# Moving waits and loads in the gradient stages of a fused attention and MLP backward kernel

## The chip, the cores and the metric

The kernel runs on one core of one Trainium2 chip. The metric is the time of one execution on the device in microseconds (us); the time before is the median of three runs. Engines are named as in the profile: PE (TensorE), DVE (VectorE), ACT (ScalarE), POOL (GpSimd) and SP (SyncE, which here only issues DMAs). Each engine works its instructions in the order in which the program lists them, and so does each engine's queue of DMA issues: an instruction that waits holds up all behind it on that engine.

## What is computed

The reference is a forward pass and its gradients (2048 tokens, width 512, 32 heads of 16, hidden width 1792, bf16):

```
x = A_x;  xn = layernorm(x)
s = attention(xn, wqkv, wo)
g = silu( gelu(layernorm(xn) @ w1 + b1) @ w2 + b2 )
out = x + s * g
_out, _vjp = jax.vjp(f, A_x, A_wqkv, A_wo, B_w1, B_b1, B_w2, B_b2)
returns out and the gradients of all seven inputs for grad_out
```

The outputs are, in order: `out` (out_0), dx (out_1), dwqkv (out_2), dwo (out_3), dw1 (out_4), db1 (out_5), dw2 (out_6), db2 (out_7).

## The kernel before

The program has three parts. `Pre` does the forward work of everything but the attention and leaves in DRAM what the gradients need. `attention_core` does scores, softmax and their gradients head pair by head pair; it takes most of the time. `Grads.run` does the rest, and the change lies in it alone. Rows of tokens are cut into 16 tiles t of 128 (NT), the width into 4 pieces of 128 (IC), the hidden width into 14 pieces fc of 128 (FC). The order of instructions is written out by hand, engine by engine, and waits follow from the tiles' uses. A new tile under an old tag waits for all uses of the old one.

`Grads.run` goes through these stages, in which every full matmul is 128x128 by 128x512:

1. **so and dwo** (t = 2 to 15). `emit_so(t)` makes four matmuls; DVE multiplies the result twice, into `dm_all` and into one of two rows "t13", which POOL adds to x one tile later (`flush_adds`) and stores from two double rows "ot". `emit_oT(t+2)` and `emit_dmT` are PE transposes into two PSUM buffers, which ACT copies out (L564, L707). `load_s1(q)` loads the factors of two tiles into one of four buffers and so waits on SP for POOL's adds of an earlier pair. At t = 9, 11, 13 and 14 `emit_dwo` makes one of four weight gradients: 16 matmuls over `Oall` and `dso_all` (L719), evacuated by ACT (L714) into one of three buffers "ob", and stored by POOL's queue.
2. **dw2** (fc = 0 to 13). `emit_dw2(fc)`: 16 matmuls (L728) over `dm_all` and `hgr[fc % 4]`, a piece of the hidden activations that a transposing DMA (`load_hg`, L698) brings in. `load_hg(fc + 4)` waits for the end of `emit_dw2(fc)`.
3. **dwq and dwkv** (i = 0 to 11). Four gradients over `xn1` and `dQall` (L812), then two halves of four over `xn1` and `dKVn[half]` (L820). Each half needs four transposing DMAs (`load_dkv`, L783). `xn1` (L800) has the buffer "xg", which `dso_all` had before.
4. **dh and dy** (four groups of each). dh needs `w2T`, 14 transposing DMAs (`load_w2T`, L780), dy needs `w1T` (L853); both change the chunks of `gp` in place or read them.
5. **dw1 and dx**. Three pieces of dw1 (L973), then 16 rows of dx (13 matmuls each, L1002 to L1006), then the last piece of dw1.

Beside stages 1 to 3 runs **slope**: the derivative of gelu for 16 chunks n of up to 128x2048, in place in `gp`. It is a list of 49 steps, which `slope_step(m)` takes m at a time. A chunk goes through a square on ACT (`sl_sq`, L654), `d1` and `d2` on DVE (two passes each, L658 to L664), two sigmoids on ACT (`sl_sg`, L668 and L669; the first one writes over `gp`, which `d2` reads) and `d3` on DVE (three passes, L673 to L675). Its inputs come through `load_h1` (L644).

A row of dx goes through `ln_a` (ACT sum L891, DVE L892 to L895, with a product tile from `row("ot")`), an ACT pass into one of four rows `r2r` (L1009), an add with the rows of grad_out, `dor` (L1011: POOL, and DVE for rows 14 and 15), and a store from SP's queue (L1014). The tile of the add comes from `row("ot")` too: that helper hands out two buffers in turn, and `ln_a` asks it once for each row as well. Ahead of the stores of rows 1 and 5 SP issues four loads each (`load_dx`).

Of the kernel before, what the change touches and what calls it, by code (L numbers as in the profile page):

```python
# [8 lines left out]
bf16 = mybir.dt.bfloat16  # L9
f32 = mybir.dt.float32  # L10
ACT = mybir.ActivationFunctionType
ALU = mybir.AluOpType
# [3 lines left out]
S, D, H, DH, F = 2048, 512, 32, 16, 1792  # L16
# [460 lines left out]
class Grads:  # L477
# [119 lines left out]
    def run(self):  # L597
        nc, k, tc, ctx = self.nc, self.k, self.tc, self.ctx
# [7 lines left out]
        ld = nc.sync.dma_start  # L606
        tr = nc.sync.dma_start_transpose
        st = nc.gpsimd.dma_start
        V = nc.vector

        def slot(tag, shape, name, dtype=bf16):
            return slots.tile(shape, dtype, name=name, tag=tag)
# [18 lines left out]
        def ob_tile():  # L631
            i = no[0] % 3
            no[0] += 1
            return slot(f"ob{i}", [128, D], "ob_w")
# [7 lines left out]
        def load_h1(tg, ci):  # L642
            c0, cn = CH[ci]
            ld(out=gpc(tg, ci), in_=h1v[:, c0:c0 + cn, tg * 512:(tg + 1) * 512])  # L644
# [43 lines left out]
        def slope_step(m=1):  # L688
            for _ in range(m):
                if slope_ops:  # L690
                    slope_ops.pop(0)[1]()
# [5 lines left out]
        def load_hg(fc):  # L697
            tr(out=hgr[:, fc % 4], in_=k.HGT_s[fc * 128:fc * 128 + 128, :])  # L698
# [4 lines left out]
        def emit_dmT(t):  # L703
            pt = self.pT([128, IC, 128], bf16, "dm_tp")
            for b in range(IC):
                nc.tensor.transpose(pt[:, b, :], dm_all[:, t, b * 128:(b + 1) * 128], k.ident_bf[:])
            nc.scalar.copy(out=dmT[:, :, t * 128:(t + 1) * 128], in_=pt[:])  # L707
            nc.tensor.matmul(psdb2[0:1, :], lhsT=ones_bf[:, 0:1], rhs=dm_all[:, t, :], start=(t == 0), stop=(t == NT - 1))

        def evac(out, in_, e):  # L710
            if e:
                nc.vector.tensor_copy(out=out, in_=in_)
            else:
                nc.scalar.copy(out=out, in_=in_)  # L714

        def emit_dwo(ac):
            ps = self.pA([128, D], f32, "ps_dwo")
            for t in range(NT):
                nc.tensor.matmul(ps[:], lhsT=k.Oall[:, t, ac * 128:(ac + 1) * 128], rhs=dso_all[:, t, :],  # L719
                                 start=(t == 0), stop=(t == NT - 1))  # L720
            ob = ob_tile()
            evac(ob[:], ps[:], 0)
            st(out=out_3[ac * 128:(ac + 1) * 128, :], in_=ob[:])

        def emit_dw2(fc):
            ps = self.pA([128, D], f32, "ps_dw2")
            for t in range(NT):
                nc.tensor.matmul(ps[:], lhsT=hgr[:, fc % 4, t, :], rhs=dm_all[:, t, :], start=(t == 0), stop=(t == NT - 1))  # L728
            ob = ob_tile()
            evac(ob[:], ps[:], 0)  # L730
            st(out=out_6[fc * 128:(fc + 1) * 128, :], in_=ob[:])
# [11 lines left out]
        for t in range(2, NT):  # L743
            self.emit_so(t)
            if t + 2 < NT:
                self.emit_oT(t + 2)
            while nd < t and nd <= 2 * (t - 3) + 1:
                emit_dmT(nd)
                nd += 1
            if t == 3:  # L750
                self.load_s1(5)
                ld(out=dso_all[:, 0:8], in_=dsov[:, 0:8])
            if t == 5:
                self.load_s1(6)
                ld(out=dso_all[:, 8:16], in_=dsov[:, 8:16])
                load_h1(0, 2)
                slope_step(1)
            if t == 7:
                self.load_s1(7)
                load_hg(0)  # L760
                slope_step(1)
            if t in (9, 11, 13, 14):
                i = (9, 11, 13, 14).index(t)
                emit_dwo(i)
                (load_hg(i + 1) if i < 3 else load_h1(1, 1))
                (load_h1(0, 3) if i == 0 else load_h1(1, 0) if i == 2 else None)
                slope_step(1 + i % 2)
        self.flush_adds()
        while nd < NT:
            emit_dmT(nd)  # L770
# [4 lines left out]
        xn1 = slot("xg", [128, NT, D], "xn1")  # L775
# [3 lines left out]
        def load_w2T(f2):  # L779
            tr(out=w2T[:, f2], in_=self.B_w2[f2 * 128:f2 * 128 + 128, :])  # L780

        def load_dkv(h, rc):
            tr(out=dKVn[h][:, :, rc, :], in_=k.dKVT_s[512 * h + rc * 128:512 * h + rc * 128 + 128, :])  # L783
# [4 lines left out]
        xnv = k.XN_s.rearrange("(t p) d -> p t d", p=128)  # L788


        nw = 0
        for fc in range(FC):
            emit_dw2(fc)
            if fc + 4 < FC:
                load_hg(fc + 4)
            if fc % 2 == 0 and fc >= 2:
                load_h1(1 + (fc + 2) // 8, ((fc + 2) // 2) % 4)
            if fc in (3, 5, 7, 9):
                q = (fc - 3) // 2
                ld(out=xn1[:, 4 * q:4 * q + 4], in_=xnv[:, 4 * q:4 * q + 4])  # L800
            if fc in (0, 2, 4, 6, 8):
                load_w2T(nw)
                nw += 1
            if fc >= 11:
                load_dkv(0, fc - 11)
            slope_step(1 + fc % 2)


        def emit_dwq(ic):
# [74 lines left out]
        def ln_a(ps, xhat, rstd_col):  # L884
            junk = self.row("oT", [128, D], bf16)
            r = self.row("t13")
            prod = self.row("ot", [128, D], bf16)
            sc = lns[nln[0] % 4] if nln[0] < 4 else slot(f"lns{nln[0] % 4}", [128, 4], "lns", f32)
            nln[0] += 1
            s1, s2, nb = sc[:, 0:1], sc[:, 1:2], sc[:, 2:3]  # L890
            nc.scalar.activation(out=junk[:], in_=ps, func=ACT.Copy, accum_out=s1)  # L891
            nc.vector.tensor_tensor_reduce(out=prod[:], in0=ps, in1=xhat, scale=-1.0 / D, scalar=0.0, op0=ALU.mult, op1=ALU.add,  # L892
                                           accum_out=s2)
            nc.vector.scalar_tensor_tensor(out=r[:], in0=xhat, scalar=s2, in1=ps, op0=ALU.mult, op1=ALU.add)
            nc.vector.tensor_scalar(out=nb, in0=s1, scalar1=-1.0 / D, scalar2=rstd_col, op0=ALU.mult, op1=ALU.mult)  # L895
            return r, nb
# [50 lines left out]
        for h4 in range(4):  # L947
            tr(out=dQT[:, 4 * h4:4 * h4 + 4].rearrange("c t b s -> c (t b) s"),
               in_=k.dQall[:, 4 * h4:4 * h4 + 4, :].rearrange("s t c -> s (t c)"))
# [5 lines left out]
        xn_all = self.pO.tile([128, NT, D], bf16, name="xn_all", tag="dQall")  # L955
        dor = slot("hgw", [128, 3, 4, D], "dor")
        r2r = slot("gp1", [128, 4, D], "r2r", f32)
        nc.vector.reduce_sum(out=db1f[:], in_=db1acc[:], axis=AX.X)

        nx = [5]  # L960
# [29 lines left out]
        def load_dx(q):  # L990
            for j in range(2):
                ld(out=R[j][:, :, 512 * q:512 * q + 512], in_=rv[:, 4 * j:4 * j + 4, 512 * q:512 * q + 512])
            ld(out=xn_all[:, 4 * q:4 * q + 4], in_=xnv[:, 4 * q:4 * q + 4])
            ld(out=dor[:, q % 3], in_=self.gov[:, q * 4:q * 4 + 4, :])
# [5 lines left out]
        for t in range(NT):  # L1000
            ps = self.pA([128, D], f32, "ps_dxa")
            nc.tensor.matmul(ps[:], lhsT=k.ident_bf[:], rhs=dxm_all[:, t, :], start=True, stop=False)  # L1002
            for cc in range(IC):
                nc.tensor.matmul(ps[:], lhsT=dQT[:, t, cc, :], rhs=wT[:, cc, :, :], start=False, stop=False)
            for rc in range(8):
                nc.tensor.matmul(ps[:], lhsT=R[rc // 4][:, rc % 4, t * 128:(t + 1) * 128], rhs=wT[:, 4 + rc, :, :], start=False, stop=(rc == 7))  # L1006
            r, nb = ln_a(ps[:], xn_all[:, t, :], k.rstd1[:, t:t + 1])
            r2 = r2r[:, t % 4, :]
            nc.scalar.activation(out=r2, in_=r[:], func=ACT.Identity, bias=nb, scale=k.rstd1[:, t:t + 1])  # L1009
            dx = self.row("ot", [128, D], bf16)  # L1010
            (V if t >= 14 else nc.gpsimd).tensor_tensor(out=dx[:], in0=r2, in1=dor[:, (t // 4) % 3, t % 4, :], op=ALU.add)  # L1011
            if t in (1, 5):
                load_dx(2 + t // 4)
            ld(out=self.o1[t * 128:(t + 1) * 128, :], in_=dx[:])  # L1014
        emit_dw1(3)


# [448 lines left out]
```

## Time and profile before

| what | value |
|---|---|
| time, median of 3 runs (lowest to highest) | 2246.61 us (2244.68 to 2248.53) |
| span of the profiled execution, first to last instruction | 2242.4 us |
| instructions | 74217 |
| PE busy | 2160.1 us (96%) |
| DVE busy | 1912.2 us (85%) |
| ACT busy | 1734.5 us (77%) |
| POOL busy | 606.8 us (27%) |
| mean granted TensorE clock | 0.991 |
| DMA moved | 461.15 MB, mean 206 GB/s |

The profiled execution's own time is given by its span; no other time of it is on record, and the median of the runs lies 4.2 us above it. The engines work beside each other, so that their busy times do not add up to the span. The shares are averages over stages with different limits; the stages that the change touches lie in the last 370 us, from about 1876 us on.

In a timeline row stand start, length, engine, line, operation, output and inputs, shape and count, and in brackets the idle time of the engine just before with what ended it. "SPq" is SP's queue of DMA issues; its length is the time that the issue held the queue, not the transfer.

### The profile page before, as it was taken

Reading aid. Unit: us, or ns where it says so; the run is one execution under the profiler, and the core shown is the slowest. Engines: PE = TensorE matmul, PEld = TensorE weight load, DVE = VectorE, ACT = ScalarE, POOL = GpSimd, SP = SyncE. Lnnn points to the kernel's source line nnn. Section 1 sums busy time; section 2 is a strip of 40 time slices with the busy share of each in tenths; the row PEclk is TensorE's granted clock in tenths of the full one; section 3 lists DMA queues with packets and bytes.
Section 4 is the critical chain, followed back from the end, with each engine's and each line's share of the span. In section 5 each row is a group of like instructions: output and inputs, shape, how many; then the busy total and the mean of one; then the engine's idle time right before and its main releaser. Section 6 shows DMA issues by size and latency. Waiting matters only on the chain.

```text
span 2242.4 us, 74217 instructions
## 1 busy us (share of the span) xinstructions
PE 2160.1 (96%) x30690; PEld 1205.0 (54%) x30690; DVE 1912.2 (85%) x3626; ACT 1734.5 (77%) x2481; POOL 606.8 (27%) x1387
## 2 busy tenths in 40 slices
PE   6998999999999999999999999999999999989996
PEld 3444555555555555555555555555555554434443
DVE  6676799999999999999999999999999997777623
ACT  4764788888888888888888888888888886674213
POOL 4276413122222222131222222221312224310012
PEclk9999899999999999999999999999999999999998
DMA  7786999999999999999999999999999999899972
GB/s 238 242 273 197 184 199 194 202 200 203 195 203 194 200 197 206 196 199 200 198 203 197 203 192 204 199 199 197 204 196 190 204 205 273 194 257 240 233 222 94
DMA packets 1421747, 461.15 MB, mean 206 GB/s; under 512 B 1334622, under 2 KB 1405662, under 8 KB 1421408
## 3 DMA queue, kind: packets, MB, share of 16 engines
q1 hardware_dynamic: 1406880, 424.67, 99.3%
q0 software_dynamic: 12944, 30.16, 5.4%
q8 instruction: 240, 3.93, 0.8%
q10 hardware_dynamic: 1584, 1.57, 0.2%
q14 instruction: 99, 0.81, 0.1%
HBM read 62.79 MB, written 64.75 MB: 57 GB/s over the span
## 4 chain that ended last, share of the span: by engine, by line
PE 86%; DMA 5%; DVE 2%; issue 2%; ACT 2%; POOL 2%; SPq 0%; POOLq 0%; DVEq 0%; ACTq 0%
PE tT L1166 23%; PE d L1104 14%; PE X L1196 10%; PE Z L1280 10%; PE X L1199 5%; PE X L1203 5%; PE s L1082 2%; PE ps_m L367 2%; PE ps_dy L902 2%; PE ps_dw L973 2%; PE ps_dh L868 2%; PE ps_h L352 2%; DMA out_dram<-ot 2%; PE XT L1222 1%; PE ps_dwkv L820 1%
## 5 line engine op out<-in xcount | busy, mean ns | idle before, releaser
L1121 DVE TENSOR_TENSOR gts<-d,ets 128x512 bf16<-128x512 f32 x2048 | 1363.2, 684 | 101.0 <-ACT ek L1178 20.3
L1091 ACT ACTIVATE ets<-s 128x1024 bf16<-128x1024 f32 x1024 | 1048.7, 1024 | 198.5 <-PE s L1082 95.2
L1166 PE MATMUL tT<-ident_bf,ets 128*128 128x128 bf16 x7168 | 568.9, 219 | 16.7 <-ACT ek L1178 6.9
L1166 PEld LDWEIGHTS <-ets 128*128 128x128 bf16 x7168 | 445.5, 97 | 242.0 <-issue 240.2
L1178 ACT COPY ek<-tT 128x448 f32<-128x448 f32 (+2 forms) x1024 | 501.6, 490 | 8.1 <-DVE ek L1178 6.9
L1104 PE MATMUL d<-QDT,KVT 32*128 32x512 bf16 x2048 | 458.6, 385 | 0.0
L1082 PE MATMUL s<-QDT,KVT 32*128 32x512 bf16 x2048 | 401.6, 381 | 3.4 <-ACT ets L1091 3.2
L1104 PEld LDWEIGHTS <-KVT 32*128 32x128 bf16 x2048 | 145.4, 91 | 323.9 <-issue 323.9
L1196 PE MATMUL X<-ets,NAT 128*32 128x256 bf16 x4096 | 300.6, 284 | 0.1
L1203 PE MATMUL X<-gts,NAT 128*17 128x256 bf16 x4096 | 290.0, 273 | 0.0
L1199 PE MATMUL X<-ets,Lc 128*32 128x256 bf16 x4096 | 289.9, 273 | 0.0
L1340 POOL COPY tick<-gts 1x2 bf16<-1x2 bf16 x205 | 36.2, 176 | 606.1 <-DVE gts L1121 606.1
L1280 PE MATMUL Z<-gk,W 128*32 128x512 bf16 x2048 | 197.8, 379 | 1.0 <-DVE acc L1294 1.0
L1280 PE MATMUL Z<-ek,W 128*32 128x512 bf16 x1792 | 198.6, 379 | 0.0
L1245 POOL TENSOR_TENSOR W<-NATQq,rL 128x128 bf16<-128x128 bf16 x64 | 25.4, 397 | 526.1 <-DVE rL L1244 443.3
L1196 PEld LDWEIGHTS <-NAT 128*32 128x32 bf16 x4096 | 106.2, 93 | 110.8 <-issue 11.4
L1082 PEld LDWEIGHTS <-KVT 32*128 32x128 bf16 x2048 | 139.0, 91 | 12.5 <-issue 9.5
L1178 DVE COPY ek<-tT 128x64 f32<-128x64 f32 (+1 forms) x576 | 132.4, 230 | 5.5 <-POOL KVT L50 4.2
L1280 PEld LDWEIGHTS <-W 128*32 128x32 bf16 x4096 | 109.7, 97 | 11.4 <-issue 1.5
L1199 PEld LDWEIGHTS <-Lc 128*32 128x32 bf16 x4096 | 107.9, 96 | 0.0
L1203 PEld LDWEIGHTS <-NAT 128*17 128x17 bf16 x4096 | 103.6, 92 | 3.1
L1280 PE MATMUL Z<-ekd,W 128*32 128x512 bf16 x256 | 97.0, 379 | 0.0
(244 smaller groups left out, 2339.3 us busy)
## 6 DMA issues: line engine op xcount, KB each, us to landing
gk<-gts SPq DMA_TRANSPOSE x512, 5.1
H1T_s<-h1r SPq DMA_DIRECT2D x28, 256.0 KB, 4.3
HGT_s<-hgT SPq DMA_DIRECT2D x8, 896.0 KB, 4.6
DH_s<-stg SPq DMA_DIRECT2D x12, 512.0 KB, 3.1
hch<-DH_s SPq DMA_DIRECT2D x12, 512.0 KB, 4.7
gp<-H1T_s SPq DMA_DIRECT2D x9, 512.0 KB, 5.4
out_dram<-ob_w POOLq DMA_DIRECT2D x36, 128.0 KB, 4.1
NAT_s<-NS SPq DMA_DIRECT2D x4, 1056.0 KB, 6.2
```

Of the source, the lines that this page charges most:

```text
L352: nc.tensor.matmul(ps[:], lhsT=w1_sb[:, ic, fc * 128:(fc + 1) * 128], rhs=yT[:, ic, g * 512:(g + 1) * 512], start=(ic == 0), stop=(ic == I ...
L367: nc.tensor.matmul(ps[:], lhsT=hgT[:, g % 2, fc, t4 * 128:(t4 + 1) * 128], rhs=w2_sb[:, fc, :], start=(fc == 0), stop=(fc == FC - 1))
L1082: nc.tensor.matmul(s[:, hj, :], lhsT=op["KVT"][r:r + 32, kb * 128:(kb + 1) * 128], rhs=op["QDT"][r:r + 32, qc * 512:(qc + 1) * 512], start ...
L1091: nc.scalar.activation(out=st_et[g][:, :, :, a[1] % 4, :].rearrange("k b h q -> k h b q"), in_=cur["s"][:].rearrange("k h (b q) -> k h b q ...
L1104: nc.tensor.matmul(d[:], lhsT=op["KVT"][r:r + 32, kb * 128:(kb + 1) * 128], rhs=op["QDT"][r:r + 32, qc * 512:(qc + 1) * 512], start=True, ...
L1121: nc.vector.tensor_tensor(out=gts[:, kb % 2, hj, :].rearrange("k (b q) -> k b q", b=4), in0=st_d.pop((g, hj))[:].rearrange("k (b q) -> k b ...
L1166: nc.tensor.transpose(t[:, i, :], et[:, b // 2, b % 2, kk, :], ident_bf[:])
L1178: copy(out=blk[j]["Ek"][kb // 4][:, kb % 4, lo:hi].rearrange("q i k -> q (i k)").bitcast(f32), in_=st_T[g][:, lo:hi].rearrange("q i k -> q ...
L1196: nc.tensor.matmul(X[r:r + 32, 0:256], lhsT=NATt[:, kb, hj, 1:33], rhs=ev, start=(kb == 0), stop=False, skip_group_check=True, tile_positi ...
L1199: nc.tensor.matmul(X[r:r + 32, 256:512], lhsT=Lc[:], rhs=ev, start=False, stop=False, skip_group_check=True, tile_position=(0, r))
L1203: nc.tensor.matmul(X[r:r + 17, 256:512], lhsT=NATt[:, kb, hj, 0:17], rhs=gv, start=False, stop=(kb == 15), skip_group_check=True, tile_pos ...
L1280: nc.tensor.matmul(Z[r:r + 32, :], lhsT=WT[j % 2][1 - part][:, qb, hj, :], rhs=mv, start=(part == 0 and qb == 0), stop=(part == 1 and qb = ...
```

## The change

Four edits, all in `Grads.run`:

- The add of a dx row writes one of eight rows of a tile of its own, `dxr`, in the buffer "gp2" (chunks that dh and dy of group 2 used before), and no longer a tile from `row("ot")`.
- In the so/dwo stage the slope steps at t = 5 and t = 7 and those behind each `emit_dwo` go; `emit_dwo` itself takes 1, 2, 1 and 2 steps between its matmuls and its evacuation. In dw2 the steps for fc = 0 to 3 are 2 each (before 1, 2, 1, 2).
- The first two of the four loads of `xn1` are issued ahead of the dw2 loop, the other two at fc = 9 and 11 (before: at fc = 3, 5, 7, 9).
- `load_w2T` is called at fc = 10 to 13 (before: fc = 0, 2, 4, 6, 8). The rest follow in the dwq/dwkv loop as before, two for each i from 4 to 8 until there are 14.

```diff
@@ emit_dwo
                 nc.tensor.matmul(ps[:], lhsT=k.Oall[:, t, ac * 128:(ac + 1) * 128], rhs=dso_all[:, t, :],
                                  start=(t == 0), stop=(t == NT - 1))
+            slope_step((1, 2, 1, 2)[ac])
             ob = ob_tile()
             evac(ob[:], ps[:], 0)
@@ loop over t
                 load_h1(0, 2)
-                slope_step(1)
             if t == 7:
                 self.load_s1(7)
                 load_hg(0)
-                slope_step(1)
             if t in (9, 11, 13, 14):
...
                 (load_h1(0, 3) if i == 0 else load_h1(1, 0) if i == 2 else None)
-                slope_step(1 + i % 2)
@@ dw2
         nw = 0
+        for q in range(2):
+            ld(out=xn1[:, 4 * q:4 * q + 4], in_=xnv[:, 4 * q:4 * q + 4])
         for fc in range(FC):
             emit_dw2(fc)
...
-            if fc in (3, 5, 7, 9):
-                q = (fc - 3) // 2
+            if fc in (9, 11):
+                q = (fc - 5) // 2
                 ld(out=xn1[:, 4 * q:4 * q + 4], in_=xnv[:, 4 * q:4 * q + 4])
-            if fc in (0, 2, 4, 6, 8):
+            if fc >= 10:
                 load_w2T(nw)
                 nw += 1
             if fc >= 11:
                 load_dkv(0, fc - 11)
-            slope_step(1 + fc % 2)
+            slope_step(1 + (fc % 2 or fc < 4))
@@ dx
+        dxr = slot("gp2", [128, 8, D], "dxr")
...
-            dx = self.row("ot", [128, D], bf16)
-            (V if t >= 14 else nc.gpsimd).tensor_tensor(out=dx[:], in0=r2, in1=dor[:, (t // 4) % 3, t % 4, :], op=ALU.add)
+            dx = dxr[:, t % 8, :]
+            (V if t >= 14 else nc.gpsimd).tensor_tensor(out=dx, in0=r2, in1=dor[:, (t // 4) % 3, t % 4, :], op=ALU.add)
...
-            ld(out=self.o1[t * 128:(t + 1) * 128, :], in_=dx[:])
+            ld(out=self.o1[t * 128:(t + 1) * 128, :], in_=dx)
```

## The prediction

> **What bounds the kernel now.** I read the page first, then the waits, the chain of waits and the timelines of the last 370 us, since the diff touches only the gradient stages after the attention loop.
>
> ```profile
> span 2242.4 us, 74217 instructions
> POOL ot L1011 <- DMA out_dram<-ot: 35.6, 13, 6.6
> DVE ot L1011 <- DMA out_dram<-ot: 11.1, 1, 11.1
> 2223.74 1.16 POOL ot L1011
> 2224.92 1.68 DMA out_dram<-ot
> 2226.82 1.16 POOL ot L1011
> 2221.96 3.54 PE L973 MATMUL ps_dw<-hch,y_all 128*128 128x256 bf16 x31 [0.29 <-DVE t L894]
> ```
>
> The waits of the last 73 us (total, times, longest) and three steps of the chain: each dx row is added on POOL into one of two "ot" buffers, but the product of `ln_a` takes every other one, so all dx rows share a single buffer. Add, store, landing, next add: 2226.82 - 2223.74 = 3.08 us a row at best, more where a load lies ahead of the store. PE's last matmul ends at 2221.96 + 3.54 = 2225.5, and 17 us of the span follow it. That is the first bound.
>
> The second is the weight-gradient stages before it, where PE sets the end but has gaps:
>
> ```profile
> 1897.90 0.38 PE L562 MATMUL o_tp<-ident_bf,Oall 128*128 128x128 bf16 x4 [3.36 <-ACT oT L564]
> 1899.42 1.89 PE L571 MATMUL ps_so<-wo_sb,oT 128*128 128x512 bf16 x4
> 1906.49 1.89 PE L719 MATMUL ps_dwo<-dso_all,Oall 128*128 128x512 bf16 x8 [0.55 <-DMA dso_all<-DSO_s]
> 1914.69 0.38 PE L562 MATMUL o_tp<-ident_bf,Oall 128*128 128x128 bf16 x4 [3.73 <-ACT oT L564]
> 1916.04 4.97 PE L719 MATMUL ps_dwo<-dso_all,Oall 128*128 128x512 bf16 x16
> 1920.85 1.03 PE L571 MATMUL ps_so<-wo_sb,oT 128*128 128x512 bf16 x4
> 1922.57 1.04 PE L571 MATMUL ps_so<-wo_sb,oT 128*128 128x512 bf16 x4
> 1936.38 34.71 PE L728 MATMUL ps_dw<-dm_all,hgr 128*128 128x512 bf16 x160
> 1972.38 3.63 PE L728 MATMUL ps_dw<-dm_all,hgr 128*128 128x512 bf16 x16 [1.29 <-DMA hgr<-HGT_s]
> 1978.32 7.28 PE L728 MATMUL ps_dw<-dm_all,hgr 128*128 128x512 bf16 x32 [2.32 <-DMA hgr<-HGT_s]
> 1988.59 3.63 PE L728 MATMUL ps_dw<-dm_all,hgr 128*128 128x512 bf16 x16 [2.99 <-DMA hgr<-HGT_s]
> 2005.87 27.79 PE L820 MATMUL ps_dwkv<-dKVn,xn 128*128 128x512 bf16 x128
> ```
>
> PE's timeline (start, length, line, count, idle before and its releaser). In the so/dwo stage (to 1936.4) two gaps of over 3 us wait for a ScalarE copy; in dw2 three gaps, 1.29 + 2.32 + 2.99 = 6.6 us, wait for transposed loads of hgr. Full speed is 34.71 / 160 = 0.217 us a matmul, so 3.47 us for a weight gradient of 16 and, from 1920.85 to 1922.57, 1.72 us for one row of so work.
>
> **Part one: dx rows in eight buffers.** Nothing is added: the same 16 adds and stores. What is late next is the layer-norm chain of ScalarE and VectorE:
>
> ```profile
> 2219.01 0.81 ACT L1009 ACTIVATE r2r<-t,lns,rstd 128x512 f32<-128x512 f32 x1 [1.73 <-DVE lns L895]
> 2222.13 0.81 ACT L1009 ACTIVATE r2r<-t,lns,rstd 128x512 f32<-128x512 f32 x1 [1.73 <-DVE lns L895]
> 2233.13 0.69 DVE L1011 TENSOR_TENSOR ot<-r2r,dor 128x512 bf16<-128x512 f32 x1 [11.10 <-DMA out_dram<-ot]
> 2236.28 0.69 DVE L1011 TENSOR_TENSOR ot<-r2r,dor 128x512 bf16<-128x512 f32 x1 [0.94 <-ACT r2r L1009]
> 2239.16 0.42 DVE L712 CAST ob_w<-ps_dw 128x256 bf16<-128x256 f32 x1 [1.85 <-DMA out_dram<-ob_w]
> ```
>
> Row 14's r2 is ready at 2222.13 + 0.81 = 2222.9; its add, which runs on VectorE, waits until 2233.13 for the store of row 13. With eight buffers it starts at about 2223.0, 10.1 us sooner. Rows come every 3.12 us (2222.13 - 2219.01), more than the 1.16 us POOL add needs, and eight rows are 25 us, longer than any store here (6.6 us was the longest wait for one), so no buffer is late again. Behind the add stand row 15, the four evacuations of dw1(3) and their stores, from 2233.13 to the end 9.3 us, all unchanged: PE's end at 2225.5 is ahead of row 15's add (2236.28 - 10.1 = 2226.2). So this part gives **10.1 us** (9 to 10.5).
>
> **Part two: slope's passes ahead of dwo's evacuation.**
>
> ```profile
> 1893.67 3.71 ACT L654 ACTIVATE sl<-gp 128x2048 bf16<-128x2048 bf16 x2 [1.19 <-DMA gp<-H1T_s]
> 1909.02 1.28 ACT L668 ACT_TABLE_LOAD   x1
> 1910.31 1.91 ACT L668 ACTIVATE gp<-sl 128x2048 bf16<-128x2048 bf16 x1
> 1912.26 1.91 ACT L669 ACTIVATE sl<-sl 128x2048 bf16<-128x2048 bf16 x1
> 1915.01 0.69 DVE L663 TENSOR_SCALAR sl<-sl 128x2048 bf16<-128x2048 bf16 x1
> 1915.73 1.23 DVE L664 TENSOR_TENSOR sl<-sl,gp 128x2048 bf16<-128x2048 bf16 x1
> 1896.30 0.46 SPq L755 DMA_DIRECT2D dso_all<-DSO_s  x1
> ```
>
> The squares (3.71 us) made the 3.36 gap; table load and sigmoids (5.1 us) made the 3.73 gap. Both now run in the shade of dwo's matmuls. Four things take part of it back.
> (1) The first gap's gain is not kept. Without it PE reaches dwo(0) at about 1898.8 (so(7) ended at 1897.90 - 3.36 = 1894.5, then two and a half rows of 1.72) and its eighth matmul at 1900.5, but the second half of dso_all, issued at 1896.30 behind a wait for POOL's add of row 5, still lands at 1906.4. PE idles 5.9 us there.
> (2) That idle time costs clock. After the 3.36 us gap four matmuls took 1.89 instead of 1.03 us, after 3.73 sixteen took 4.97 instead of 3.63; after 2.99 sixteen took 3.63, undisturbed. From 1914.69 to 1920.85 PE took 6.16 us for half a row (0.85) and sixteen matmuls (3.47): 1.8 us lost to the clock. So, the same taken here, dwo(0) ends near 1910.0, not 1908.2. [...]
> (3) dwo(1) then runs 1913.4 to 1916.9, but sigmoid(0) on ScalarE waits for d2(0) on VectorE: so(11) ends at 1912.6, two products of 0.69 (the 128x512 add's row), then 0.69 + 1.23, to 1915.9. It runs 3.8 us, to 1919.7, and behind it queue the evacuation and the copy of oT(14) on ScalarE (0.55 each, an estimate between the rows of 0.42 and 0.69), and POOL's store and next add. PE needs oT(14)'s buffer for oT(15) at 1919.5 and gets it at 1920.8: 1.3 us.
> (4) At dwo(3), from 1927.0, VectorE has so(14)'s products (1926.4 to 1927.8), d2(1) (1.9) and d3(0) (1.23 + 0.69 + 1.23 = 3.15) ahead of so(15)'s product, done at 1933.5; dmT(15), which needs it, could start at 1932.2: 1.3 us.
> Adding rows of 1.72 and blocks of 3.47 through these waits, dw2 starts at 1934.1 instead of 1936.4: **2.3 us** (0.5 to 4.5). Slope steps done by dw2(3) are 14 both ways (8+6 before, 6+8 after), so nothing is owed later.
>
> **Part three: loads around dw2.**
>
> ```profile
> 1943.49 5.57 SPq L698 DMA_TRANSPOSE hgr<-HGT_s  x2
> 1956.00 0.58 SPq L800 DMA_DIRECT2D xn<-XN_s  x1
> 1991.73 8.02 SPq L783 DMA_TRANSPOSE dKVn<-dKVT_s  x3
> 2011.39 4.55 SPq L783 DMA_TRANSPOSE dKVn<-dKVT_s  x1
> 2015.99 5.19 SPq L780 DMA_TRANSPOSE w2T<-in_B_w_dram  x4
> DMA to landing us min/median/max: 5.5/6.4/7.1
> 1892.00:1908.00 16.00, 11.99 (x68) 5.69 (x66) 9.88 (x13) 8.47 (x11) 7.76 (x8) 0.89 1.07 392
> 1921.00:1936.00 15.00, 13.84 (x81) 6.51 (x78) 12.89 (x15) 11.23 (x13) 7.50 (x9) 1.00 0.42 143
> 1952.00:1992.00 40.00, 33.37 (x153) 14.43 (x152) 31.00 (x36) 29.10 (x24) 5.26 (x9) 1.00 1.18 254
> ```
>
> SP's queue, the landing of dKVn, and three stretches (last columns: clock, DMA share, GB/s). From 1952 on DMA is full (share 1.18); from 1921 to 1936 it is not (0.42), and SP waits for dw2(0). The first two xn quarters (1 MB) go into that hole: they wait on SP for dwo(3)'s end, and what queues behind them, hgr(4), waits for dw2(0) anyway. Ahead of hgr(13) three xn loads and five w2T transposes leave the queue; what remains per weight gradient is one transpose (5.57 / 2 = 2.8 us) and half a gp load (between 0.3 us of issue and, at 392 GB/s, 0.7 us) against PE's 3.47. hgr(fc+4) goes out when dw2(fc) ends and is needed 3 x 3.47 = 10.4 us later; at a landing like dKVn's 6.4 that leaves 4 us, more than a lag of at most 0.3 us each over nine loads takes. So the **6.6 us** of dw2's gaps go.
>
> But the same queue then feeds dwkv, which needs all four dKVn transposes of a half. Now the four w2T (5.19 / 4 = 1.3 us each) and two xn loads stand ahead of them. Before, the last of half 0 went out near 1991.73 + 2 x 2.67 = 1997.1 and landed 6.4 later, 2003.5, against PE at 2005.87; the last of half 1 at 2011.39 + 6.4 = 2017.8 against 2005.87 + 13.81 = 2019.7: 1.9 us in hand (1.2 to 2.8 by the landing's ends). The queue's work between is the same but for the two xn quarters, worth 0.6 to 1.3 us each, say 2.0 together; it starts 2.3 us sooner; PE's pace idles it perhaps 0.5 us early in dw2. So dKVn comes 3.8 us sooner, and PE can gain at most 3.8 + 1.9 = **5.7 us** here, not 2.3 + 6.6 = 8.9: about 3 us come back as waits for dKVn, short enough to cost no clock. Ends: 2.4 (0.5 + 1.2 - 0.5 + 1.2) and 8.9.
>
> After that the queue has one w2T more (1.3 us) ahead of w1T, which dy needs only behind eight chunks of dh: nothing, or 1.3 if that cover fails.
>
> **Sum.** 5.7 + 10.1 = 15.8 us off a span of 2242.4: 2226.6. The median of the runs, 2246.6, is 4.2 us above the profiled span; I keep that distance: **2230.8 us**, own range 2227 to 2234.
>
> **Rivals.**
> *dKVn does not bind.* If the transposes ran closer to plain loads, both halves are there in time and the PE stages give 8.9: 2246.6 - 19.0 = 2227.6. For: copies and transposes overlap in places. Against: 2.67 to 2.8 us a transpose back to back, where 512 KB at 392 GB/s are 1.34. [...] 0.17.
> *The PE stages bring nothing.* The wait at dso_all and dKVn's lateness, one above 3.3 us with its 1.8 us of cold clock, eat the 5.7: only the tail's 10.1 is left, 2236.5. For: both waits follow from rows. 0.15.
> *The eight buffers act as one.* If the add of a row still waited for the store before it, because the tile is tracked as a whole, only 5.7 stay: 2240.9. Against: r2r, cut by rows in the same way, is written by ScalarE while POOL still owes older rows. 0.05.
> *Slower.* Between hgr(13), issued near 1971, and half 1, eight dKVn and four w2T transposes queue. At 4.55 us each, the slowest of the rows above, for all twelve (54.6 us, with 3.5 us for the loads between them and 6.4 of landing), half 1 lands at about 2035.5 instead of 2017.8; PE loses 15.8 there and the tail gives 10.1: 2252.3. It decides once that landing passes 2019.7 + 10.1 = 2029.8. Against: three in a row took 8.02. 0.03.
>
> **How the numbers follow.** Forecast 0.60, rivals 0.17, 0.15, 0.05, 0.03. The range, 2225.5 to 2237, takes in the first two rivals and the bounds of parts two and three, and leaves out the last two with the forecast's tails. 0.2% is 4.5 us, about what a measurement here tells from no change. All cases but the last are faster by more; the one-buffer case is so by only 1 us, so part of it goes to "same": 0.95, 0.02, 0.03.
>
> **What would show it.** Right: no wait of POOL or VectorE at L1011 for a store; row 14's add within 0.2 us of its r2; the span ending 7 us after PE, not 17; no gap at oT(9), one of about 6 us in the middle of dwo(0) with slow matmuls behind it; no hgr gaps, and waits of 1 to 4 us ahead of the two halves of dwkv. Wrong: L1011 still waiting for DMA, hgr gaps that stay, or a dwkv wait over 6 us.

## The result and the profile after

| kernel | median (lowest to highest), us | ratio to before, 95% interval |
|---|---|---|
| before, same chip | 2244.68 (2242.73 to 2248.53) | |
| after | 2232.33 (2229.55 to 2238.35) | 0.9940 (0.9927 to 0.9954) |

The change makes the kernel 12.35 us faster, where 15.8 were forecast. The median lies 1.5 us above the 2230.8 of the prediction. Part of that nearness is luck: the kernel before came out at 2244.68 here, 1.9 us under the 2246.61 that the forecast starts from, and the sum behind it did not come out term by term.

To see the terms, I divided both traces, and that of every experiment, at the first matmul of each stage on PE. The count starts at so(2), the first so of the loop, because the attention ahead of it, which no kernel here changes, ended anywhere from 1882.1 to 1892.4 us in the profiled executions. What is left from there to the end of the span is what the edits can move. All values are in us. Kernels below "after" are the experiments. Each row is one execution.

| kernel | so/dwo | dw2 | dwq and dwkv | dh to dy and dw1 | dx to the end | from so(2) on |
|---|---|---|---|---|---|---|
| before | 52.64 | 55.67 | 41.44 | 139.52 | 69.39 | 358.66 |
| after | 53.62 | 48.36 | 45.24 | 139.52 | 58.97 | 345.71 |
| dx alone | 52.64 | 54.79 | 41.44 | 139.52 | 58.96 | 347.35 |
| slope alone | 53.63 | 54.85 | 41.44 | 139.51 | 67.75 | 357.18 |
| loads alone | 53.43 | 48.36 | 47.79 | 139.52 | 69.43 | 358.53 |
| dx and loads | 54.10 | 48.36 | 45.63 | 139.51 | 58.94 | 346.54 |
| dso_all early, gp late | 51.02 | 48.36 | 46.96 | 139.52 | 58.93 | 344.79 |
| w2T late | 55.38 | 50.02 | 41.44 | 139.52 | 58.90 | 345.26 |
| both | 51.74 | 48.35 | 43.24 | 139.52 | 58.97 | 341.82 |
| both, d2 early | 50.84 | 48.36 | 42.66 | 139.52 | 58.96 | 340.34 |
| dso_all and gp at the start | 47.06 | 48.36 | 41.43 | 139.52 | 58.89 | 335.26 |
| the same, table early | 44.00 | 48.36 | 41.43 | 139.53 | 58.95 | 332.27 |
| the same, d3 early again | 47.35 | 48.36 | 41.66 | 139.51 | 58.94 | 335.82 |
| after, table early | 52.51 | 50.23 | 47.10 | 139.53 | 59.20 | 348.57 |

So after minus before, from so(2) on: so/dwo +0.98, dw2 -7.31, dwq and dwkv +3.80, dx -10.42, together -12.95. The span itself fell by 14.6; the other 1.65 is the attention, which ended at 1882.09 instead of 1883.74. The table also shows how far executions of the same code differ: so/dwo took 52.64 to 54.10 us in the four kernels with slope's steps as before (before, dx alone, loads alone, dx and loads), and 53.62 to 55.38 in the three with the steps of the change (after, slope alone, w2T late). The +0.98 lies within that scatter, the -7.31 and -10.42 far outside.

The tail in the trace of after: its span from the page, POOL's wait for the adds of dx from the view of waits (total, times, longest), then the timelines of PE, ACT and DVE.

```profile
span 2227.8 us, 74213 instructions
POOL dxr L1012 <- ACT r2r L1010: 27.9, 13, 4.5
2213.72 7.38 PE L974 MATMUL ps_dw<-hch,y_all 128*128 128x256 bf16 x64
2217.73 0.81 ACT L1010 ACTIVATE r2r<-t,lns,rstd 128x512 f32<-128x512 f32 x1 [1.73 <-DVE lns L895]
2218.57 0.69 DVE L1012 TENSOR_TENSOR dxr<-r2r,dor 128x512 bf16<-128x512 f32 x1 [0.94 <-ACT r2r L1010]
2224.60 0.42 DVE L712 CAST ob_w<-ps_dw 128x256 bf16<-128x256 f32 x1 [1.85 <-DMA out_dram<-ob_w]
```

The add now waits for ACT's r2 and for no store. Row 14's add starts at 2218.57, right after its r2 (2217.73 + 0.81 = 2218.54), where before it waited 11.10 us. PE ends at 2213.72 + 7.38 = 2221.1 and the span 6.7 us later instead of 17.

PE's timeline in the so/dwo stage of after, and the stretch 1899 to 1912 in the view of windows (length; PE, PEld, DVE, ACT, POOL busy; granted clock; DMA share; GB/s):

```profile
1899.48 2.95 PE L719 MATMUL ps_dwo<-dso_all,Oall 128*128 128x512 bf16 x8 [2.40 <-DMA dso_all<-DSO_s]
1905.47 3.57 PE L719 MATMUL ps_dwo<-dso_all,Oall 128*128 128x512 bf16 x8 [3.04 <-DMA dso_all<-DSO_s]
1908.83 1.80 PE L571 MATMUL ps_so<-wo_sb,oT 128*128 128x512 bf16 x4
1921.98 0.38 PE L562 MATMUL o_tp<-ident_bf,Oall 128*128 128x128 bf16 x4 [2.73 <-ACT oT L564]
1935.07 0.40 PE L706 MATMUL dm_tp<-ident_bf,dm_all 128*128 128x128 bf16 x4 [2.00 <-DVE dm_all L573]
1899.00:1912.00 13.00, 9.48 (x33) 3.56 (x33) 3.21 (x4) 3.97 (x5) 3.59 (x4) 0.61 1.07 308
```

The two ScalarE gaps of before have made room for four others. Both halves of `dso_all` are late, each is followed by eight slow matmuls (2.95 and 3.57 us, 1.89 at full clock), and the clock of the stretch is 0.61.

PE's timeline from dw2 to dh in after:

```profile
1937.66 46.57 PE L729 MATMUL ps_dw<-dm_all,hgr 128*128 128x512 bf16 x215
1984.07 13.98 PE L812 MATMUL ps_dwq<-dQall,xn 128*128 128x512 bf16 x64
1999.67 13.97 PE L820 MATMUL ps_dwkv<-dKVn,xn 128*128 128x512 bf16 x64 [1.63 <-ACT ob_w L714]
2015.50 13.97 PE L820 MATMUL ps_dwkv<-dKVn,xn 128*128 128x512 bf16 x64 [1.86 <-DMA dKVn<-dKVT_s]
```

dw2 runs without a gap, 0.217 us a matmul. Each half of dwkv starts late. The releaser named in the third row, an evacuation on ACT, had long been done: PE works with five result buffers here, and the one it needed was free from 1985.6 on, the end of the last evacuation of dw2 (1985.06 + 0.57). As in the fourth row it is the transposed load that comes last.

### The profile page after: what moved, and what is told of

The parts are those of the page before. It is cut to its first block, busy times and chain, and to the rows that moved or that the text cites. A ratio compares the mean times of both kernels' runs of the same rounds, so it can differ in the third digit from the quotient of the medians.

```text
span 2227.8 us, 74213 instructions
## 1 busy us (share of the span) xinstructions
PE 2158.9 (97%) x30690; PEld 1204.8 (54%) x30690; DVE 1912.6 (86%) x3626; ACT 1734.3 (78%) x2481; POOL 607.5 (27%) x1387
## 4 chain that ended last, share of the span: by engine, by line
PE 89%; DVE 3%; DMA 3%; ACT 3%; issue 2%; SPq 1%; POOL 1%; DVEq 0%; ACTq 0%; POOLq 0%
PE tT L1167 24%; PE d L1105 14%; PE X L1197 10%; PE Z L1281 10%; PE X L1200 5%; PE X L1204 5%; PE s L1083 2%; PE ps_dw L729 2%; PE ps_dy L902 2%; PE ps_m L367 2%; PE ps_h L352 2%; PE ps_dw L974 2%; PE ps_dh L868 2%; PE XT L1223 1%; PE ps_qkv L210 1%
```

## The experiments

### The change in three parts

Each of the four kernels is the kernel before with only some of the edits of the diff.

```diff
dx alone:       +dxr = slot("gp2", [128, 8, D], "dxr")   (and its use)
slope alone:    +slope_step((1, 2, 1, 2)[ac])   (and the steps that go)
loads alone:    +if fc in (9, 11): ...  +if fc >= 10:   (xn1 and w2T)
dx and loads:   the first and the third
```

> The kernel before with the eight dx buffers alone. Theory (the layer-norm chain is next): from the first dx matmul to the end 59.0 us instead of 69.4, no wait of POOL or VectorE for a store at the add, all stages ahead as before; 10.4 us off, about 2234.3. Rival (the gain also needs the other edits, since the loads of the dx stage move with them): under 8 us off.

> The kernel before with the slope steps moved alone. Theory (the gaps come back as the wait for both halves of dso_all, cold clock, the table load and POOL's add behind the dwo store): so/dwo, from so(2) to dw2's start, 53.6 us instead of 52.6, the dw2 gaps of 6.6 us stay; time within 1.5 us of before. Rival, the step as the prediction sized it: so/dwo 50.3 us, 2.3 us off.

> The kernel before with the xn and w2T loads moved alone. Theory (dKVn binds after dw2): dw2 48.4 us instead of 55.7 from its start to dwq's, then 3 to 4 us of waits ahead of the two halves of dwkv; 3.5 us off, about 2241. Rival (dKVn was late only because the slope edit shifted the queue): no dwkv waits, 7.3 us off.

> Eight dx buffers and the moved loads, slope as in the kernel before. Theory (the slope edit loses 1.0 us by itself and the parts add up): 13.9 us off, about 2230.8, 0.5 to 1.5 us faster than the whole change. Rival (the slope edit helps elsewhere, for example by starting dw2's steps sooner): slower than the whole change by over 1 us.

Measured: dx alone 2237.99 us (2236.80 to 2238.08), ratio 0.9963 (0.9950 to 0.9976); slope alone 2248.58 (12 runs), 1.0011 (0.9997 to 1.0026); loads alone 2244.90 (11 runs), 0.9987 (0.9976 to 0.9998); dx and loads 2236.61 (6 runs), 0.9954 (0.9941 to 0.9968). The kernel before was 2247.21 in this set.

The dx edit alone gives the whole of the tail, 69.39 to 58.96; its median is 9.2 us off where 10.4 were expected. The loads alone take dw2 to 48.36 and give it back in dwkv: 47.79 instead of 41.44, so that from so(2) to dh hardly anything is left (149.58 against 149.75). With dx beside them they kept 1.7 us against before and 0.8 against dx alone (148.09 against 148.87). The slope edit alone brings nothing: its so/dwo stage takes 53.63 us, and kernels without it took 52.64 to 54.10.

The time of dx and loads missed its expectation: 10.6 us off instead of 13.9, and not faster than the whole change. The interval overlaps that of the change, so whether the slope edit is worth something beside the other two stays open; by the medians it is 1.8 us (10.6 against 12.35), by the traces from so(2) on 0.8.

### Both halves of dso_all ahead of the loop

```diff
-        load_h1(0, 0)
-        load_h1(0, 1)
+        ld(out=dso_all[:, 0:8], in_=dsov[:, 0:8])
+        ld(out=dso_all[:, 8:16], in_=dsov[:, 8:16])
 ...  (at t == 3, behind load_s1(5))
-                ld(out=dso_all[:, 0:8], in_=dsov[:, 0:8])
+                load_h1(0, 0)
+                load_h1(0, 1)
 ...  (at t == 5)
-                ld(out=dso_all[:, 8:16], in_=dsov[:, 8:16])
```

> The whole change, with both halves of dso_all issued ahead of slope's first two chunks, so behind no wait for POOL's add. Theory (the freed gaps went into the wait for dso_all and the cold clock behind it, 2.40 + 3.04 of gap and 3.5 of slow matmuls): no gap at dwo(0), clock 1.00 there, so/dwo 53.6 - 9 = 44 to 46 us. Of that the dKVn waits take some back, since DMA starts sooner only by what its own queue allows: total 3 to 8 us faster than the whole change. Rival (ScalarE's chain, table load to oT(14), sets the stage): so/dwo still over 50 us.

Measured: 2230.50 us (2228.66 to 2231.98), ratio 0.9935 (0.9919 to 0.9952), no different from the change itself. PE's timeline, and ACT's first squares:

```profile
1909.70 0.38 PE L562 MATMUL o_tp<-ident_bf,Oall 128*128 128x128 bf16 x4 [1.91 <-ACT oT L564]
1921.47 0.58 PE L562 MATMUL o_tp<-ident_bf,Oall 128*128 128x128 bf16 x4 [2.76 <-ACT oT L564]
1904.98 3.71 ACT L654 ACTIVATE sl<-gp 128x2048 bf16<-128x2048 bf16 x2 [2.71 <-DMA gp<-H1T_s]
```

No gap waits for `dso_all` any more, but now the squares wait 2.71 us for the `gp` chunks that I moved out of the way, and hold up the copy of oT behind them. The stage takes 51.02 us; the 44 to 46 of the theory failed, and the rival, the chain through ScalarE, takes over most of the gap. The late load was one wait among several of about the same size.

### w2T behind dKVn

```diff
-            if fc >= 10:
-                load_w2T(nw)
-                nw += 1
 ...  (dwq and dwkv, 4 <= i <= 8)
-                for _ in range(2):
+                for _ in range(3):
```

> The whole change, with no w2T transpose ahead of dKVn: three for each i from 4 to 8 of the dwq/dwkv loop. Theory (four w2T of 1.3 us in front of dKVn make the two waits ahead of dwkv, 1.8 + 2.0): both waits under 0.5 us, 3 to 4 us faster. Rival (DMA as a whole is full, order does not matter): the waits go elsewhere, w2T late at dh, under 1 us gained.

Measured: 2229.31 us (2228.73 to 2232.25), ratio 0.9935 (0.9920 to 0.9950). PE's timeline of dw2 and dwkv, and SP's queue:

```profile
1938.42 50.18 PE L729 MATMUL ps_dw<-dm_all,hgr 128*128 128x512 bf16 x224
2002.25 27.79 PE L817 MATMUL ps_dwkv<-dKVn,xn 128*128 128x512 bf16 x128
1988.12 7.87 SPq L781 DMA_TRANSPOSE dKVn<-dKVT_s  x3
```

dwkv runs its 128 matmuls in one piece, and dh is not late for it (139.52 us from dh on, as before). This execution alone leaves a rival: PE also came to dwkv later, since it lost 1.76 us more in so/dwo and 1.66 in dw2 than after. The two kernels with dso_all and gp at the start, below, take that rival out: there dw2 takes 48.36 us as in after, and dwkv waits for nothing either (41.43 from dwq on). So the four transposes of w2 ahead of dKVn were what made it late in the changed kernel. The 3 to 4 us expected do not show in the total. The 224 matmuls of dw2 took 50.18 us without a gap where they took 48.52 in the fastest kernel: the granted clock from 1937 to 1990 is 0.97, behind a gap of 2.00 us ahead of dmT(15).

### Both together, and d2 earlier

"Both" has the two edits above. "d2 early" has in addition:

```diff
-            slope_step((1, 2, 1, 2)[ac])
+            slope_step((1, 1, 1, 2)[ac])
+            if t == 10:
+                slope_step(1)
```

> Both of the last two edits. Theory: so/dwo 44 to 46 us and waits ahead of dwkv of 0 to 4 us, since PE comes 8 us sooner than DMA; 6 to 11 us faster than the whole change. Rival (DMA full from 1886 on): no more than the better of the two alone.

> As the last, with slope's step d2(0) taken at t = 10 rather than in dwo(1), so that the first sigmoid's table load does not wait for VectorE behind so(11). Theory (ScalarE waited 2.1 us for d2 in dwo(1), and the evacuation, oT(14), POOL's store and add stood behind it): the gap of 2.7 us ahead of oT(15) falls under 0.5 us, 2 to 2.7 us faster than the last. Rival (the sigmoids' 5.1 us alone outlast dwo(1)'s 3.5): the gap stays over 1.5 us.

Measured: both 2227.48 us (6 runs), ratio 0.9929 (0.9910 to 0.9948); with d2 early 2226.79 (2224.20 to 2230.88), 0.9923 (0.9906 to 0.9940). Both expectations failed: so/dwo takes 51.74 us instead of 44 to 46, and the medians are not told apart from the change by their intervals. From so(2) on the two executions take 341.82 and 340.34 us, against the 345.71 of the change. Waits for the second half of dKVn, 1.80 and 1.22 us, stay here, and at most 0.22 in the later kernels; why they differ stays open. d2 early took the gap at oT(15) from 4.44 to 2.04 us, where under 0.5 was expected, and the gap at oT(13) grew from 2.50 to 3.21:

```profile
1914.15 2.70 DVE L664 TENSOR_TENSOR sl<-sl,gp 128x2048 bf16<-128x2048 bf16 x1
1914.60 1.16 POOL L584 TENSOR_TENSOR ot<-t,s1b 128x512 bf16<-128x512 f32 x1
```

These are d2(0)'s second pass on DVE, 2.70 us instead of 1.23, and the add on POOL beside it: at t = 10 the pass is earlier, but meets an add.

### dso_all and gp both at the start, d3 out of the way

```diff
+        ld(out=dso_all[:, 0:8], in_=dsov[:, 0:8])
+        ld(out=dso_all[:, 8:16], in_=dsov[:, 8:16])
         load_h1(0, 0)
         load_h1(0, 1)
 ...  (emit_dwo; w2T behind dKVn and d2(0) at t = 10 as above)
-            slope_step((1, 1, 1, 2)[ac])
+            slope_step((1, 1, 1, 1)[ac])
 ...  (dw2)
-            slope_step(1 + (fc % 2 or fc < 4))
+            slope_step(1 + (fc % 2 or fc < 4) + (fc == 0))
```

The second kernel adds one early activation, on a column that is filled with zeros:

```diff
                 self.load_s1(6)
+                nc.scalar.activation(out=warm[:, 1:2], in_=warm[:, 0:1], func=ACT.Sigmoid)
```

> The changed kernel with both halves of dso_all and with the gradient chunks h1(0,0) and h1(0,1) all issued ahead of the loop over the row tiles, d2(0) at t = 10, one slope step ahead of each dwo store (so that d3(0) and the second Sigmoid come in the dw2 loop), and the transposes of w2 behind those of dKVn. Theory (four terms of the stage so/dwo: late dso_all, late squares, sigmoid chain, d3(0) ahead of the product of so(15)): the gaps ahead of dwo(0) and at the copies behind the squares go, the 2.0 us gap ahead of dmT(15) goes; what is left is the gap at oT(15), 0.8 to 2.0 us. Stage so/dwo 47 to 49 us (50.84 in the run with d2 early, 53.62 in the changed kernel), dw2 48.4, dwq 13.8, dwkv 28.9 to 29.5, dx 59.0; from so(2) to the end 336.5 to 338.5 us. Rival (VectorE, slowed by GpSimd's adds, sets the pace whatever the loads and the order): stage so/dwo 50 to 51 us, from so(2) to the end 339.5 to 341.

> As the run before it, with one Sigmoid on a single column at t = 5, whose result nobody reads, so that the table for Sigmoid is loaded there and not in the chain d1(0), Sigmoid, evacuation. Theory (the table load waits with its activation and so stands in the chain): no ACT_TABLE_LOAD near 1915; the gap at oT(15) becomes shorter by 1.28 us or goes; stage so/dwo 46 to 48 us, 0.8 to 1.5 us less than the run before it. Rival (the load at t = 5 holds up a copy of oT by the same 1.28 us and another gap opens there): stage so/dwo the same within 0.4 us, and a gap of about 1 us at so(7) or so(8).

Measured: the first 2224.99 us (2222.83 to 2225.62), ratio 0.9896 (0.9876 to 0.9917); the second 2221.94 (2220.53 to 2230.43), 0.9891 (0.9871 to 0.9910). That is below the change's own interval, and from so(2) on the second takes 332.27 us, 13.4 less than the change. It is the fastest version here. ACT and PE of the first kernel, then PE of the second:

```profile
1914.89 1.28 ACT L668 ACT_TABLE_LOAD   x1 [2.68 <-issue]
1921.05 0.59 PE L562 MATMUL o_tp<-ident_bf,Oall 128*128 128x128 bf16 x4 [3.32 <-ACT oT L564]
1922.56 5.59 PE L719 MATMUL ps_dwo<-dso_all,Oall 128*128 128x512 bf16 x16
```

```profile
1902.46 3.63 PE L719 MATMUL ps_dwo<-dso_all,Oall 128*128 128x512 bf16 x16
1919.15 0.39 PE L562 MATMUL o_tp<-ident_bf,Oall 128*128 128x128 bf16 x4 [2.44 <-ACT oT L564]
1920.26 3.63 PE L719 MATMUL ps_dwo<-dso_all,Oall 128*128 128x512 bf16 x16
1930.49 0.40 PE L706 MATMUL dm_tp<-ident_bf,dm_all 128*128 128x128 bf16 x4 [0.26 <-DVE dm_all L573]
```

In both dwo(0) runs in one piece, and the gap ahead of dmT(15) is 0.26 us. So the 47 to 49 us expected of the first from four terms came (47.06), and the rival's 50 to 51 fell; of the terms, the gap at oT(15) was missed, 3.32 us and slow matmuls behind it where 0.8 to 2.0 us were expected. The early table load brought 3.06 us, more than the 0.8 to 1.5 expected. Only 0.88 of them are the shorter gap at oT(15). 1.96 are the clock of the dwo behind it, which takes 3.63 us instead of 5.59 (granted clock 0.80 from 1912 to 1925 and 0.95 from 1925 to 1940 in the first, 1.00 in both stretches in the second), and the early load alone does not secure them (d3 early, next, has the same load and a slow dwo there). The rest is mostly a gap of 1.16 us at an earlier dmT that went, one of 0.71 at oT(13) that came, and 0.41 us more for the row of so at t = 7, since copies on ACT now stand behind the load.

### d3 early again, and the table load alone

```diff
 d3 early:  -slope_step((1, 1, 1, 1)[ac])   +slope_step((1, 1, 1, 2)[ac])   (and the extra step in dw2 goes)
 table:     the changed kernel with the early Sigmoid and nothing else
```

> The run with the early table load (stage so/dwo 44.0 us), with two slope steps instead of one ahead of the last dwo store, as in the run with d2 early: d3(0) and the second Sigmoid stand ahead of the product of so(15) on VectorE again. Theory (that order alone made the 2.00 us gap ahead of dmT(15)): a gap of 1.9 to 2.1 us ahead of dmT(15), stage so/dwo 45.9 to 46.1 us, or up to 47.7 where TensorE's clock falls behind the gap. Rival (the gap came from a late chain, and goes with it): no gap there, stage so/dwo 43.9 to 44.4 us.

> The changed kernel with nothing but the one-column Sigmoid at t = 5, whose result nobody reads. Theory (the table load stands in the chain d1(0), Sigmoid, evacuation there too): no ACT_TABLE_LOAD near 1915, gap at oT(15) 1.2 to 1.7 us instead of 2.73, stage so/dwo 51.9 to 52.6 us instead of 53.62. Rival (in the changed kernel the late dso_all and the cold clock set the end of the chain, and the load lies beside them): gap at oT(15) 2.5 us or more, stage so/dwo 53.2 to 53.9 us.

Measured: d3 early 2224.79 us (2 runs), ratio 0.9893 (0.9864 to 0.9922); the changed kernel with the early table 2235.41 (2231.62 to 2242.78), 0.9938 (0.9927 to 0.9949), beside 2249.24 for the kernel before in this set. PE of the first, then PE of the second:

```profile
1919.42 0.38 PE L562 MATMUL o_tp<-ident_bf,Oall 128*128 128x128 bf16 x4 [2.35 <-ACT oT L564]
1920.81 4.93 PE L719 MATMUL ps_dwo<-dso_all,Oall 128*128 128x512 bf16 x16
1934.10 0.40 PE L706 MATMUL dm_tp<-ident_bf,dm_all 128*128 128x128 bf16 x4 [2.01 <-DVE dm_all L573]
```

```profile
1931.21 0.38 PE L562 MATMUL o_tp<-ident_bf,Oall 128*128 128x128 bf16 x4 [1.30 <-ACT oT L564]
```

The order on DVE alone brings back the gap ahead of dmT(15), 2.01 us, as the theory had it. The stage is 3.35 us longer, since 1.30 us of clock in the dwo above it (4.93 against 3.63; granted clock 0.89 from 1920 to 1936 against 1.00) and a gap of 1.07 us at an earlier dmT came on top, while the gap of 0.71 at oT(13) went. Of the two kernels before it, the one without the early table has a gap of 1.16 us at that dmT too, and the one with it none, which stays unexplained. In the changed kernel the early table takes the gap at oT(15) from 2.73 to 1.30 us and the stage from 53.62 to 52.51, as expected. The total does not show it: dw2 behind it took 50.23 us instead of 48.36, without a gap, and dKVn came later still (47.10 for dwq and dwkv).

## Why the prediction was right, and where its steps were not

**The tail.** Right in every step: 10.42 us against 10.1, shown alone by the first experiment. The eight buffers do not act as one. With the old rows the stage scatters more (67.75 to 69.43 us in three executions) than with the new (58.89 to 59.20 in eleven), so that its worth is 8.6 to 10.5 us by execution.

**dw2.** Right: the three gaps went, 7.31 us against 6.6. The one transpose and half a load that stay for each weight gradient fit into PE's 3.47 us.

**dKVn.** Right in kind, and near in size: 3.80 us came back against about 3. The nearness is in part luck, since the four other kernels with the same loads gave back 4.2 to 6.4. The queue's rows in after, of the last two transposes of the first half and the four of the second:

```profile
1991.33 5.25 SPq L781 DMA_TRANSPOSE dKVn<-dKVT_s  x2
1997.31 4.10 SPq L781 DMA_TRANSPOSE dKVn<-dKVT_s  x1
2002.07 6.49 SPq L781 DMA_TRANSPOSE dKVn<-dKVT_s  x2
2009.24 3.28 SPq L781 DMA_TRANSPOSE dKVn<-dKVT_s  x1
```

The rival by which dKVn does not bind is thereby out: in the five kernels that have the edits of the loads and keep w2T ahead of dKVn, dwq and dwkv take 3.8 to 6.4 us more than 41.44, and in the six that move w2T behind it 0 to 1.8, none of it ahead of the first half. Nor did the transposes in after run near the pace of plain loads: two of them, of 512 KB each, together held the queue for 6.49 us, beside other loads and stores. At the 392 GB/s of the prediction's busiest stretch 512 KB are 1.34 us.

**so/dwo.** This step failed: 2.3 us were to go, none went, and 0.98 came on top in the traced execution, which is within the scatter. Measured from so(2) it is 3.3 us off there, and the four take-backs of the prediction carry all of it. Rows of after, of SP, ACT, DVE and POOL:

```profile
1894.02 0.46 SPq L756 DMA_DIRECT2D dso_all<-DSO_s  x1
1914.52 1.23 DVE L664 TENSOR_TENSOR sl<-sl,gp 128x2048 bf16<-128x2048 bf16 x1
1915.83 1.28 ACT L668 ACT_TABLE_LOAD   x1 [2.09 <-DVE sl L664]
1921.74 0.57 POOL L724 DMA_DIRECT2D out_dram<-ob_w  x1 [7.81 <-ACT ob_w L714]
1922.34 1.17 POOL L584 TENSOR_TENSOR ot<-t,s1b 128x512 bf16<-128x512 f32 x1
1923.54 0.69 DVE L575 TENSOR_TENSOR t<-ps_so,s1w 128x512 f32<-128x512 f32 x1 [3.56 <-POOL ot L584]
1924.15 2.13 DVE L658 TENSOR_SCALAR sl<-sl 128x2048 bf16<-128x2048 bf16 x1
1924.55 1.17 POOL L584 TENSOR_TENSOR ot<-t,s1w 128x512 bf16<-128x512 f32 x1
1934.33 0.68 DVE L573 TENSOR_TENSOR dm_all<-ps_so,s1w 128x512 bf16<-128x512 f32 x1
```

- (1) `dso_all`: 5.9 us of idling forecast in the middle of dwo(0); measured 2.40 + 3.04 = 5.44, in two places, because the first half was late too. Off by -0.5.
- (2) The clock: 1.8 us forecast. Beside full-speed rows (1.89, 1.89, 1.03) the eight, eight and four matmuls lost 1.06 + 1.68 + 0.77 = 3.5. Two gaps cost clock twice. Off by +1.7, of this execution: in w2T late the same stage took 55.38 us, and the granted clock from 1900 to 1937 was 0.82 instead of 0.86 in after.
- (3) The wait at oT(15): 1.3 us forecast, 2.73 measured. I had let the table load of 1.28 us run ahead of time, as in the trace of before it seemed to; it waits with its activation for d2(0) and starts where that ends (1914.52 + 1.23). With the load taken out of the chain the gap is 1.30 us. Off by +1.4.
- (4) The wait at dmT(15): 1.3 us forecast, 2.00 measured. What is queued behind the evacuation is longer than I had it: POOL's dwo store waits for it, the add behind that store frees the row that DVE's next product needs, and d1(1) starts at 1924.15 and takes 2.13 us instead of 0.69 beside POOL's next add. So so(15)'s product starts only at 1934.33, and dmT(15) waits for it. Off by +0.7.

The terms add to 3.3. That several waits of the same size stand behind each other is shown by the experiments: `dso_all` early alone made room for the squares' wait, and only with all of them removed or shortened did the stage fall to 44.00 us.

**The sum.** PE's stages gave 2.5 us (149.75 to 147.22 from so(2) to dh) where 5.7 were forecast, the tail 10.4. With the measured so/dwo in the prediction's own sum for dKVn, the queue starts 3.3 us later than forecast and 3.8 - 3.3 + 1.9 = 2.4 us are left (an estimate), close to the 2.5 measured: the one failed step carries the miss of the PE stages. The 4.2 us between span and median that the forecast kept came out as 4.5, by chance: the traced execution's own time is 1.75 us above its span (2229.55 against 2227.8), and it was the shortest of the five. Without the slope edit the gain would have been about the same: dx and loads together take 346.54 us from so(2) on, the whole change 345.71.

## What to carry to other kernels

Where an engine's order is written by hand, work that is moved under a long matmul still stands ahead of that block's evacuation, and the evacuation stands ahead of a store, an add and a product on three other engines: follow that chain round to the block that needs its end before counting the shade as free. Where several waits of 1 to 3 us have nearly the same end, removing the last one yields only the distance to the next, so count them all and remove them together. A load that goes from a full queue is a gain only if what it is moved in front of has time in hand; here the transposes of w2 were not needed before dh, and those of dKVn had about two microseconds in hand.

## What the runs showed of the hardware

**The clock did not go by the length of a gap alone.** PE's rows and windows of the kernel with dx and loads, behind a gap of 2.00 us:

```profile
2001.50 15.66 PE L822 MATMUL ps_dwkv<-dKVn,xn 128*128 128x512 bf16 x63 [2.00 <-DMA dKVn<-dKVT_s]
2001.50:2005.50 4.00, 4.00 (x11) 1.48 (x12) 0.55 (x2) 1.91 (x1) 0.23 (x1) 0.58 1.12 280
2005.50:2010.00 4.50, 4.45 (x21) 2.08 (x21) 4.40 (x6) 2.66 (x4) 0.72 (x1) 0.99 1.02 238
```

The granted clock was 0.58 for 4 us, then 0.99. Two rows shown above make it plainer still: at the same place of the program a gap of 2.35 us was followed by a dwo of 4.93 us and one of 2.44 us by a dwo of 3.63. Why like gaps end differently no run here shows. The prediction took waits of this size to cost no clock, since a gap of 2.99 us had cost none; that held for dKVn's waits in after, and not here. For the sum it means that a gap of about 2 us or more in these stages was followed here by a loss of another 1 to 2.5 us, or by none: 1.06 followed 2.40 and 2.45 followed 3.04 in after, and none followed 2.73.

**Two of VectorE's bf16 passes took 1.4 to 1.5 us longer beside one of GpSimd's adds.** A pass of 0.69 us took 2.13, and one of 1.23 took 2.70, with one add of 1.17 and 1.16 us on POOL in that time (1924.55, and 1914.60 in the kernel with d2 early). It also went the other way; in after an add took 1.70 us instead of 1.17 beside a pass that kept its 1.23:

```profile
1900.29 1.23 DVE L659 TENSOR_TENSOR sl<-sl,gp 128x2048 bf16<-128x2048 bf16 x1
1900.82 1.70 POOL L584 TENSOR_TENSOR ot<-t,s1x 128x512 bf16<-128x512 f32 x1 [1.67 <-DVE sl L658]
```

Why they lengthen each other no run here shows. The prediction took the durations of passes that ran alone.

**The table load was paid for where it cost less.** One Sigmoid on a single column moved the 1.28 us out of the chain, to 1895.89 in the fastest kernel, and no second load appeared behind it there. It was not free: in the two kernels that have it beside dso_all and gp at the start, the row of so at t = 7 took PE 2.13 us instead of 1.72.
